# q and k transposed before the launch, first heads' operands written in place, half of the probabilities' low parts queued behind the next row maximum

## The chip, the cores and the metric

The kernel runs on one core of a Trainium2 chip. The metric is the device time of one execution in microseconds (us), taken as the median of several runs. Five engines are named by the profile: PE (matmul; PEld is its weight load), DVE (vector), ACT (scalar), POOL (GpSimd) and SP, which only issues DMAs here. Each engine works through its own instructions in order and waits for others on semaphores.

## The reference, cut to what matters

The program computes an attention in which a query sees only the keys of its own hash bucket, then a mixture of experts with the best expert alone, then a dense layer with ELU. Only the attention is touched by the change. There are 2 batches of 8 heads, 768 positions and 64 dimensions per head; `proj` is 64 by 6.

```
q_bits = (einsum('bhsd,dk->bhsk', q, proj) > 0)       # 6 bits
k_bits = (einsum('bhsd,dk->bhsk', k, proj) > 0)
q_bucket, k_bucket = sum(bits * 2 ** arange(6))
mask = q_bucket[:, :, :, None] == k_bucket[:, :, None, :]
scores = where(mask, q @ k.T / 8, -1e9)
attn = softmax(scores);  attn_out = attn @ v
x = moe(attn_out as [1536, 512]);  out = elu(x @ w_in) @ w_out
```

All values are 32-bit floats. PE multiplies them in a shorter form, so the kernel splits each operand into a high part (the value rounded to that form) and a low part (the value less its high part) and multiplies the parts.

## The kernel before

**Tiles.** The 16 heads are worked as 8 pairs. A head has 6 query tiles of 128 rows, so there are 96 tiles (NQ) and 12 per pair (s = 0 to 11). One trip of the loop over n (lines 951 to 1007) issues, for different tiles, one step of each stage. The order in which the code issues is the order in which each engine works; nothing is rescheduled. A trip issues:

- stage_M(n-1), lines 360 to 370: DVE takes the row maximum `nm` of the scores of tile n-1 out of PSUM, POOL makes a scale `sc` and a bias `bi` of it.
- what was put in the list `early` by the trip before.
- stage_T(n-3), lines 384 to 401: PE turns the probabilities in two halves of 3 blocks (tile `t`, from a PSUM pool of 3 buffers, tag "t"); ACT writes the high part `pthi` and DVE the low part `ptlo` of each half.
- `late[0]`, the first half of a preparation step (below).
- stage_S(n), lines 342 to 353: PE makes the scores `s` by 4 matmuls of 384 columns.
- stage_R, lines 472 to 517, in two trips of twelve: PE brings finished head outputs back into token order by 6 matmuls, DVE scales them.
- stage_V, lines 405 to 415: PE multiplies `pthi` and `ptlo` with v by 4 matmuls (tile `o`).
- stage_E(n-1), lines 372 to 380: ACT takes the exponential of the scores with bias and scale, into `p`.
- stage_O once in three trips: ACT copies `o` out.
- `late[1]`, the second half of a preparation step.
- what the table `todo` has for this trip.

**Mask.** The bucket test is part of the score matmul. The operands are stacked: `qa` holds high and low part of q, `ka` the high part of k twice; `qb` and `kb` hold q's high and k's low part in rows 0 to 63 and, from row 64 on, rows built from the hash bits, so that equal buckets add the large constant UNIT (line 20) and others less. MROWS (line 22) is the number of those rows.

**Preparation of a pair.** While pair pr is worked, the next pair is prepared in 6 steps (lines 994 to 997: at s = 1, 2, 4, 5, 7, 8). Steps 0 to 3 are prep_T (lines 204 to 227), one for each half of 384 positions of q and of k: PE turns three 128x128 blocks of the raw rows (`prep`, PSUM, tag "t"), ACT writes the high part (`qhi`, `khi`), DVE the low part (`qlo`, `klo`). Steps 4 and 5 are prep_Z (lines 273 to 292): 4 matmuls with the projection (`zps`, tag "t"), ACT copies half of the result (`zb`), DVE compares (`z`). restack (lines 294 to 318) then copies the parts to the stacked operands by DMAs on SP's queue. PE, which issues in order, works a step's transposes between stage_V and the next stage_T.

**Start.** Lines 621 to 668 prepare the first pair before the first tile: `load_pair` brings q and k with 64 values in a row of a head, PE turns them, and the first head's operands are copied into their places by ACT, POOL and DMAs. keep_warm issues matmuls without a use.

## Time and profile before

| what | value |
| --- | --- |
| time, median of 3 runs | 712.68 us (712.56 to 712.94) |
| the profiled execution's own time | 713.77 us |
| its span, first to last instruction | 712.0 us |
| first row maximum, that of tile 0 | starts at 10.35 us |
| last row maximum, that of tile 95 | starts at 244.72 us |
| granted TensorE clock, mean | 0.997 |

The 96 tiles thus take a third of the span; what follows (experts, dense layer) is the other two thirds. The rows of the trace that the prediction uses are shown further down. A PE row's duration is longer than the time until the next matmul may start, since matmuls overlap; so on PE the distance from start to start is what counts.

### The profile page before, as it was taken

How to read it: one execution, taken by the hardware profiler on the slowest of the kernel's cores; microseconds unless marked ns; L12 is line 12 of the kernel's file. 1: busy time of each engine (PE TensorE's matmuls, PEld its weight loads, DVE VectorE, ACT ScalarE, POOL GpSimd, SP SyncE). 2: the span in 40 equal slices, each digit the busy share in tenths (PEclk: the TensorE clock that was granted, in tenths of full speed). 3: DMA queues.
4: the chain of work that ended last, by engine and by line, in shares of the span. 5: the costliest groups of instructions: out<-in, count | busy, mean ns of one | idle time of the engine just before them, and what ended most of it. 6: DMA issues, size and time to landing. Idle time of an engine off the chain costs nothing.

```text
span 712.0 us, 12226 instructions
## 1 busy us (share of the span) xinstructions
PE 698.5 (98%) x4211; PEld 626.8 (88%) x4212; DVE 553.7 (78%) x1046; ACT 428.4 (60%) x855; POOL 211.1 (30%) x508
## 2 busy tenths in 40 slices
PE   8999999999999999999999999999999999999996
PEld 6899999999998988999999998788888888888884
DVE  6989898899998997788888887877788547934433
ACT  6988888888888865666666665445443224422221
POOL 7665445455456661221065311000000000002012
PEclk9999999999999999999999999999999999999998
DMA  8857758686691239788878986322222000001011
GB/s 188 198 136 178 186 129 210 163 189 164 144 233 57 84 116 299 239 261 242 261 209 247 256 217 144 104 88 75 89 87 92 2 0 1 0 1 60 0 60 62
DMA packets 108596, 97.39 MB, mean 137 GB/s; under 512 B 33480, under 2 KB 94728, under 8 KB 108528
## 3 DMA queue, kind: packets, MB, share of 16 engines
q1 hardware_dynamic: 106064, 90.15, 47.3%
q0 software_dynamic: 2304, 6.40, 2.4%
q8 instruction: 35, 0.57, 0.3%
q14 instruction: 33, 0.27, 0.1%
q10 hardware_dynamic: 160, 0.00, 0.0%
HBM read 64.15 MB, written 10.72 MB: 105 GB/s over the span
## 4 chain that ended last, share of the span: by engine, by line
issue 32%; PE 23%; DMA 6%; POOL 1%; ACT 0%; SPq 0%; POOLq 0%; ACTq 0%
PE hps L1135 11%; PE yps L1148 7%; DMA out_dram<-part,tidt 5%; PE yps L1150 3%; DMA xs<-xs_d 1%; PE xTp L1117 1%; DMA tidt<-tid_d 1%; PE yps L1147 0%; POOL xs L857 0%; POOL out_dram L1293 0%; ACT sum L1153 0%; POOL spacer L612 0%; SPq L743 0%; POOLq L1293 0%; ACTq L1153 0%
## 5 line engine op out<-in xcount | busy, mean ns | idle before, releaser
L399 DVE TENSOR_TENSOR ptlo<-t,pthi 128x384 fp32r<-128x384 f32 x192 | 99.9, 548 | 14.7 <-ACT pthi L398 13.1
L376 ACT ACTIVATE p<-s,bi,sc 128x768 f32<-128x768 f32 x96 | 95.9, 999 | 17.5 <-POOL bi L369 15.7
L832 DVE TENSOR_TENSOR wl<-wraw,wh 128x1024 fp32r<-128x1024 f32 (+1 forms) x65 | 77.4, 1194 | 23.7 <-ACT wh L828 21.4
L367 DVE TENSOR_REDUCE nm<-s 128x1 f32<-128x768 f32 x96 | 90.9, 947 | 0.3 <-PE s L349 0.3
L398 ACT ACTIVATE pthi<-t 128x384 fp32r<-128x384 f32 x192 | 84.8, 497 | 10.2 <-PE t L396 8.9
L1293 POOL DMA_INDIRECT out_dram<-part,tidt x12 | 11.5, 960 | 263.5 <-DVE part L1290 262.2
L1255 ACT ACTIVATE ee<-gps 128x512 f32<-128x512 f32 x48 | 28.7, 597 | 98.0 <-PE gps L1245 98.0
L1148 PE MATMUL yps<-h,wh 128*128 128x448 f32 x256 | 84.4, 380 | 0.0
L396 PE MATMUL t<-ident,p 128*128 128x128 f32 x576 | 79.5, 273 | 0.0
L1245 PE MATMUL gps<-x2h,vl 128*128 128x512 f32 x192 | 75.9, 395 | 0.0
L1275 PE MATMUL a<-vh,gh 128*128 128x512 f32 x192 | 75.6, 394 | 0.0
L1275 PE MATMUL a<-vh,gl 128*128 128x512 f32 x192 | 75.4, 393 | 0.0
L1245 PE MATMUL gps<-x2h,vh 128*128 128x512 f32 x192 | 75.3, 392 | 0.0
L1245 PE MATMUL gps<-x2l,vh 128*128 128x512 f32 x192 | 75.2, 392 | 0.0
L1275 PE MATMUL a<-vl,gh 128*128 128x512 f32 x192 | 74.9, 390 | 0.0
L349 PE MATMUL s<-ka,qa 128*128 128x384 f32 x192 | 73.4, 383 | 1.2 <-DMA qa<-qlo 0.4
L1258 ACT ACTIVATE gh<-ee 128x512 fp32r<-128x512 f32 x48 | 30.4, 633 | 69.2 <-DVE ee L1257 69.2
L1256 DVE TENSOR_SCALAR ee<-ee 128x512 f32<-128x512 f32 x48 | 20.4, 426 | 66.3 <-ACT ee L1255 66.2
L396 PEld LDWEIGHTS t<-ident,p 128*128 128x128 f32 x576 | 67.4, 140 | 3.9 <-DVE ptlo L399 0.5
L828 ACT ACTIVATE wh<-wraw 128x1024 fp32r<-128x1024 f32 x63 | 66.2, 1052 | 2.7 <-DMA wraw<-in_moe_w_dram 2.7
L413 PE MATMUL o<-pthi,vst 128*128 128x384 f32 x192 | 66.9, 349 | 0.3
L349 PE MATMUL s<-kb,qb 102*128 102x384 f32 x192 | 65.3, 341 | 0.4 <-DMA kb<-z 0.4
(224 smaller groups left out, 1768.8 us busy)
## 6 DMA issues: line engine op xcount, KB each, us to landing
wraw<-in_moe_w_dram SPq DMA_DIRECT2D x64, 512.0 KB
w<-in_moe_w_in_dram SPq DMA_DIRECT2D x16, 512.0 KB
w<-in_moe_w_out_dram SPq DMA_DIRECT2D x16, 512.0 KB
ka<-khi SPq DMA_DIRECT2D x30, 192.0 KB
xs_d<-zt SPq DMA_DIRECT2D x8, 528.0 KB
xs<-xs_d SPq DMA_DIRECT2D x8, 528.0 KB
...
```

Source lines behind the costliest of these rows:

```text
L349: nc.tensor.matmul(ps[:, j, 0:HC], opnd[st, "q" + x][0:n1, cb], opnd[st, "k" + x][0:n1, j * HC:(j + 1) * HC], start=(x == "a"), stop=(x == ...
L367: nc.vector.tensor_reduce(nm, sps[n][:, :, 0:HC], AX.XY, ALU.max, negate=True)
L376: nc.scalar.activation(p.rearrange("p (a b) -> p a b", a=2), sps.pop(n)[:, :, 0:HC], AF.Exp, bias=bi, scale=sc, accum_out=sums[hd][:, c:c ...
L396: nc.tensor.transpose(ps[:, a, :], p[:, kt * 128:(kt + 1) * 128], ident)
L398: nc.scalar.activation(ho, ps, AF.Copy)
L399: nc.vector.tensor_tensor(lo[:, HALF * g:HALF * (g + 1), i * 128:(i + 1) * 128], ps, ho, ALU.subtract)
L413: nc.tensor.matmul(ops[m], vst[hd][:, kt, :], t[:, kt, :], start=(kt == 0 and x == 0), stop=(kt == NC - 1 and x == 1))
L832: fs = [lambda c=slice(j, j + h): eng.tensor_tensor(lo[:, c], r[:, c], hi[:, c], ALU.subtract) for j in range(0, PW, h)]
L1135: nc.tensor.matmul(ps, w[:, dc, fs], x[:, dc], start=(i == 0), stop=(i == len(terms) - 1))
L1148: nc.tensor.matmul(ps, wh[:, f], h[:, :, f], start=(f == 0), stop=last)
L1245: nc.tensor.matmul(ps, w[:, dc], x[:, dc, th * TC:(th + 1) * TC], start=(dc == 0 and i == 0), stop=(dc == KD - 1 and i == 2),)
L1275: nc.tensor.matmul(ps, x[:, cs], w, start=(fb in first_fb and i == 0), stop=(fb in last_fb and i == 2))
```

## The change

1. **Layout from the host.** `kernel()` hands q and k over as [batch, head, 64, 768], with positions in the order in which the tiles use them, and `proj` twice over. prep_T has no transposes: its source is the raw SBUF tile, and ACT and DVE read that in place of PSUM. A pair's q or k is one DMA of 128 rows of 3 KB, in place of two with pieces of 256 bytes.
2. **Start.** The first two heads (0 and 1) get loads of their own (`load_one`). Their high and low parts are written straight into the stacked operands, head by head, by ACT, DVE and POOL; no restack DMA is needed for them. Their hash is taken from the stacked operands with 2 matmuls per operand and stretch in place of 3. Head 1 is done in trips 1 to 4 through `todo`.
3. **Mask rows.** MROWS goes from 38 to 18; restack of the bits takes 2 DMAs per head in place of 3.
4. **Preparation steps.** They are spread by a table to at most one per trip: from the second prepared pair on, the four high parts come at s = 0, 1, 4 and 6, the low parts two trips after the call, ahead of stage_T's, and prep_Z at s = 3 and 7. stage_R comes one trip later (s = 8 and 11).
5. **Low parts.** Of the two `ptlo` of a tile, the second is put in `lows_t` and issued in the next trip, behind stage_M.

```
@@ load_pair @@
-                t = ap2.tile([128, NC, 2 * D], F32, tag="raw_" + nm, name="raw_" + nm, bufs=2 if nm == "q" else 1)
-                step = HALF if pr == 0 else NC
-                for c0 in range(0, NC, step):
-                    for hh in range(2):
-                        nc.sync.dma_start(
-                            t[:, c0:c0 + step, hh * D:(hh + 1) * D],
-                            src[b, h0 + hh].rearrange("(p c) d -> p c d", c=NC)[:, c0:c0 + step],
-                        )
+                t = ap2.tile([128, S], F32, tag="raw_" + nm, name="raw_" + nm, bufs=2 if nm == "q" else 1)
+                nc.sync.dma_start(t, src[b, h0:h0 + 2].rearrange("h d s -> (h d) s"))
@@ prep_T @@
-        r = raw[pr, nm]
-        ps = prep_psum("prep")
-        for c in range(HALF):
-            cc = HALF * j + c
-            nc.tensor.transpose(ps[:, c * 128:(c + 1) * 128], r[:, cc, :], ident)
         sl = slice(j * HC, (j + 1) * HC)
-        sc = 1.0 / float(D) ** 0.5 / UNIT
+        ps = raw[pr, nm][:, sl]
+        sc = SCALE
...
@@ the first two heads @@
+    def key_low(hd, j):
+        o, h = (opnd[hd, t][0:64, half(j)] for t in ("kb", "ka"))
+        nc.vector.tensor_tensor(o, one[hd, "k"][:, half(j)], h, ALU.subtract)
+    def query_low(hd, c0, c1):
+        cs = slice(c0, c1)
+        t = opnd[hd, "qa"]
+        nc.vector.scalar_tensor_tensor(t[64:128, cs], one[hd, "q"][:, cs], SCALE, t[0:64, cs], ALU.mult, ALU.subtract)
+    def hash_of(ps, hd, nm, cs, start=True, stop=True):
+        a = opnd[hd, nm + "a"]
+        w, t = (1, a) if nm == "q" else (2 + hd, opnd[hd, "kb"])
+        m = ps.shape[0]
+        nc.tensor.matmul(ps, bdr[:, w - 1 if nm == "q" else w, 0:m], a[:, cs], start=start, stop=False)
+        nc.tensor.matmul(ps, bdr[0:64, w, 0:m], t[0:64, cs], start=False, stop=stop)
...
@@ stage_T @@
-            nc.vector.tensor_tensor(lo[:, HALF * g:HALF * (g + 1), i * 128:(i + 1) * 128], ps, ho, ALU.subtract)
+            po = lo[:, HALF * g:HALF * (g + 1), i * 128:(i + 1) * 128]
+            if g and later:
+                lows_t.append(lambda: nc.vector.tensor_tensor(po, ps, ho, ALU.subtract))
+            else:
+                nc.vector.tensor_tensor(po, ps, ho, ALU.subtract)
@@ prep, and the table of steps @@
+    def prep(pr, nm, j):
+        high, low = prep_T(pr, nm, j)
+        highs.append(high)
+        early.append(lambda: early.append(low))
...
+            else ((-1, "q", 0), (0, "k", 0), (3, "q", 1), (5, "k", 1))
...
+        for j, n in enumerate((6, 8) if p == 1 else (3, 7)):
+            at(n0 + n, prep_Z, p, j)
@@ the loop @@
         if 1 <= n < NQ + 1:
             stage_M(n - 1)
+        both(lows_t)
+        lows_t.clear()
         stage_A(n)
-        both(early)
-        early = []
+        now, early[:] = early[:], []
+        both(now)
         if 3 <= n < NQ + 3:
             m, part = divmod(n - 5, HALF)
-            stage_T(n - 3, (lambda: stage_G2(m)) if m >= 0 and part == 0 else None)
+            stage_T(n - 3, n < NQ, (lambda: stage_G2(m)) if m >= 0 and part == 0 else None)
...
-        m, part = divmod(n - 13, HALF)
+        m, part = divmod(n - (14 if n < NQ - 12 else 13), HALF)
@@ kernel() @@
+        if name in ("q", "k"):
+            b, h, t, d = a.shape
+            a = a.reshape(b, h, 128, t // 128, d).transpose(0, 1, 4, 3, 2).reshape(b, h, d, t)
```

What moves on the engines is seen in their instruction orders. On PE, in a trip of the loop with a preparation step, before the change (`prep` is the preparation's PSUM tile, `t` the turned probabilities, `s` the scores, `o` the product with v):

```order
L212 MATMUL prep<-ident,raw_k 128x128 x3
L396 MATMUL t<-ident,p 128x128 x6
L349 MATMUL s<-ka_142,qa_140 128x384
L349 MATMUL s<-kb_143,qb_141 128x384
L349 MATMUL s<-ka_142,qa_140 128x384
L349 MATMUL s<-kb_143,qb_141 128x384
L413 MATMUL o<-pthi,vst 128x384
L413 MATMUL o<-ptlo,vst 128x384
L413 MATMUL o<-pthi,vst 128x384
L413 MATMUL o<-ptlo,vst 128x384
```

And PE in such a trip now:

```order
L433 MATMUL t<-ident,p 128x128 x6
L384 MATMUL s<-ka_128,qa_126 128x384
L384 MATMUL s<-kb_129,qb_127 128x384
L384 MATMUL s<-ka_128,qa_126 128x384
L384 MATMUL s<-kb_129,qb_127 128x384
L454 MATMUL o<-pthi,vst 128x384
L454 MATMUL o<-ptlo,vst 128x384
L454 MATMUL o<-pthi,vst 128x384
L454 MATMUL o<-ptlo,vst 128x384
```

The three transposes of the preparation are gone, and nothing stands in their place.

On DVE, two trips of the loop before (`nm` is the maximum, `ptlo` the low part of the turned probabilities, `ri` a reciprocal, `qlo` a low part of the next pair):

```order
L367 TENSOR_REDUCE nm<-s 128x1
L399 TENSOR_TENSOR ptlo<-t,pthi 128x3x128
L460 RECIPROCAL ri<-sm 128x3
L399 TENSOR_TENSOR ptlo<-t,pthi 128x3x128
L221 SCALAR_TENSOR_TENSOR qlo<-prep,qhi 128x384
L367 TENSOR_REDUCE nm<-s 128x1
L399 TENSOR_TENSOR ptlo<-t,pthi 128x3x128 x2
L221 SCALAR_TENSOR_TENSOR qlo<-prep,qhi 128x384
```

And DVE now, two trips (line 438 is the second `ptlo`, put off from the trip before, line 440 the first of its own trip):

```order
L402 TENSOR_REDUCE nm<-s 128x1
L438 TENSOR_TENSOR ptlo<-t,pthi 128x3x128
L223 SCALAR_TENSOR_TENSOR qlo<-raw_q,qhi 128x384
L440 TENSOR_TENSOR ptlo<-t,pthi 128x3x128
L402 TENSOR_REDUCE nm<-s 128x1
L438 TENSOR_TENSOR ptlo<-t,pthi 128x3x128
L225 TENSOR_TENSOR klo<-raw_k,khi 128x384
L440 TENSOR_TENSOR ptlo<-t,pthi 128x3x128
```

One `ptlo` of a tile has moved from ahead of the next maximum to behind it, and the preparation's low part reads SBUF (`raw_q`) where it read PSUM (`prep`).

On DVE at the start, from the first maximum on, before:

```order
L367 TENSOR_REDUCE nm<-s 128x1
L221 SCALAR_TENSOR_TENSOR qlo<-prep,qhi 128x384
L367 TENSOR_REDUCE nm<-s 128x1
L251 TENSOR_SCALAR qb_129<-zps,thr,amp 38x384
L258 TENSOR_SCALAR z<-zps 128x384
L367 TENSOR_REDUCE nm<-s 128x1
L399 TENSOR_TENSOR ptlo<-t,pthi 128x3x128 x2
L258 TENSOR_SCALAR z<-zps 128x384
L367 TENSOR_REDUCE nm<-s 128x1
```

And now (`kb_129` and `qa_126` are operands of head 1, `qb_123` of head 0):

```order
L402 TENSOR_REDUCE nm<-s 128x1 x2
L282 TENSOR_SCALAR qb_123<-zps,thr,amp 18x384
L246 TENSOR_TENSOR kb_129<-kr,ka_128 64x384
L402 TENSOR_REDUCE nm<-s 128x1
L440 TENSOR_TENSOR ptlo<-t,pthi 128x3x128
L261 SCALAR_TENSOR_TENSOR qa_126<-qr,qa_126 64x384
L246 TENSOR_TENSOR kb_129<-kr,ka_128 64x384
L402 TENSOR_REDUCE nm<-s 128x1
L438 TENSOR_TENSOR ptlo<-t,pthi 128x3x128
L293 TENSOR_SCALAR z<-zps 50x384
L440 TENSOR_TENSOR ptlo<-t,pthi 128x3x128
L261 SCALAR_TENSOR_TENSOR qa_126<-qr,qa_126 64x384
```

Head 1's low parts, four instructions of 64x384, now stand between the first maxima, where before one low part of 128x384 stood there for both heads.

## Rows read from the trace of the kernel before

**Rows 1.** The page: busy time, share, instructions; granted clock in 40 slices.
```profile
PE 698.5 (98%) x4211; PEld 626.8 (88%) x4212; DVE 553.7 (78%) x1046; ACT 428.4 (60%) x855; POOL 211.1 (30%) x508
...
PEclk9999999999999999999999999999999999999998
```

**Rows 2.** Windows of pairs 3 and 7: length, then busy PE, PEld, DVE, ACT, POOL.
```profile
67.68:97.46 29.78, 29.78 (x201) 28.84 (x201) 26.84 (x51) 26.13 (x58) 14.77 (x47) 1.00 0.74 186
...
187.38:217.97 30.59, 30.47 (x216) 29.06 (x215) 28.07 (x66) 26.61 (x60) 15.43 (x50) 1.00 0.69 178
```

**Rows 3.** Timeline, PE alone, tiles 24 to 28: start, duration, engine, line.
```profile
66.72 0.42 PE L349 MATMUL s<-ka,qa 128*128 128x384 f32 x1
...
68.81 0.45 PE L349 MATMUL s<-ka,qa 128*128 128x384 f32 x1
...
70.33 0.49 PE L212 MATMUL prep<-ident,raw_q 128*128 128x128 f32 x3
...
70.66 0.82 PE L396 MATMUL t<-ident,p 128*128 128x128 f32 x6
...
71.23 0.42 PE L349 MATMUL s<-ka,qa 128*128 128x384 f32 x1
...
73.64 0.42 PE L349 MATMUL s<-ka,qa 128*128 128x384 f32 x1
...
75.95 0.44 PE L349 MATMUL s<-ka,qa 128*128 128x384 f32 x1
```

**Rows 4.** Groups by line, PE: count, busy us, mean ns.
```profile
L212 PE MATMUL prep<-ident,raw_k 128*128 128x128 f32 x48 | 8.2, 282 | 0.1
L212 PE MATMUL prep<-ident,raw_q 128*128 128x128 f32 x48 | 7.9, 273 | 0.7 <-DMA raw_q<-in_q_dram 0.5
```

**Rows 5.** Timeline, DVE and ACT, tiles 24 to 26.
```profile
67.25 1.02 DVE L399 TENSOR_TENSOR ptlo<-t,pthi 128x384 fp32r<-128x384 f32 x2 [0.18 <-ACT pthi L398]
...
67.68 0.99 ACT L376 ACTIVATE p<-s,bi,sc 128x768 f32<-128x768 f32 x1
...
68.19 0.95 DVE L367 TENSOR_REDUCE nm<-s 128x1 f32<-128x768 f32 x1
...
68.74 0.87 ACT L398 ACTIVATE pthi<-t 128x384 fp32r<-128x384 f32 x2
...
72.71 0.55 DVE L221 SCALAR_TENSOR_TENSOR qlo<-prep,qhi 128x384 fp32r<-128x384 f32 x1
...
73.18 0.95 DVE L367 TENSOR_REDUCE nm<-s 128x1 f32<-128x768 f32 x1
```

**Rows 6.** Timeline, PE and DVE, tiles 31 and 32, which hold stage_R and prep_Z.
```profile
83.10 0.45 PE L349 MATMUL s<-ka,qa 128*128 128x384 f32 x1
...
83.74 0.34 PE L349 MATMUL s<-kb,qb 102*128 102x384 f32 x1
...
84.54 0.95 DVE L367 TENSOR_REDUCE nm<-s 128x1 f32<-128x768 f32 x1
...
86.70 0.42 PE L349 MATMUL s<-ka,qa 128*128 128x384 f32 x1
...
88.36 0.95 DVE L367 TENSOR_REDUCE nm<-s 128x1 f32<-128x768 f32 x1
```

**Rows 7.** Timeline, the start: first transposes, maxima of tiles 0 and 12.
```profile
4.34 0.85 PE L212 MATMUL prep<-ident,raw_k 128*128 128x128 f32 x3
...
10.35 0.96 DVE L367 TENSOR_REDUCE nm<-s 128x1 f32<-128x768 f32 x1 [0.31 <-PE s L349]
...
37.76 0.95 DVE L367 TENSOR_REDUCE nm<-s 128x1 f32<-128x768 f32 x1
```

**Rows 8.** Timeline, DVE instructions with two SBUF inputs, and POOL beside them.
```profile
258.23 0.92 POOL L873 TENSOR_SCALAR sel<-ranks,row 128x224 fp32r<-128x224 bf16 x1 [1.12 <-DVE row L863]
258.35 0.94 DVE L883 SCALAR_TENSOR_TENSOR xlo<-xw,xhi 128x512 fp32r<-128x512 f32 x1
...
259.46 0.74 DVE L883 SCALAR_TENSOR_TENSOR xlo<-xw,xhi 128x512 fp32r<-128x512 f32 x1
```

271 lines of the change are left out of this document (146 added, 125 removed).

## The prediction

> **What bounds the kernel now.** I read the page first, then one window per pair of heads, then the timeline of a few trips of the loop. The page gives the granted clock at nine tenths or more in all forty slices and PE busy for 98% of the span, DVE 78%, ACT 60% [rows 1]. So PE is the engine to doubt first, but its busy time overstates it, because matmul rows overlap. The windows show what the attention looks like by itself: in pair 3 PE is busy for the whole 29.78 us, DVE for 26.84, ACT for 26.13; in pair 7 DVE has risen to 28.07 of 30.59 [rows 2]. Three engines are near full, so taking work from one can hand the bound to the next.
>
> The timeline settles which it is. From the first score matmul of one tile to that of the next takes 68.81 − 66.72 = 2.09 us in a plain trip and 71.23 − 68.81 = 2.42, then 73.64 − 71.23 = 2.41, in trips that hold a preparation step [rows 3]. The three transposes of that step start at 70.33 and the next work starts at 70.66: 0.33 us, exactly the difference [rows 3]. A trip with stage_R and one prep_Z takes 86.70 − 83.10 = 3.60 [rows 6], 1.51 over a plain one. A whole pair is 12 × 2.09 + 4 × 0.33 + 2 × 1.51 = 29.42, against 29.78 in its window [rows 2]: PE's own work explains all but 0.36 us. Part of that rest is seen: the trip from 73.64 to 75.95 has no extra work on PE and yet takes 2.31 [rows 3]. It is the trip that has a high part on ACT and a low part on DVE to catch up with.
>
> **Term 1, the transposes.** They go without a substitute on PE. There are 48 for k and 48 for q in the run [rows 4], 12 per pair. The first pair's 12 belong to the start; the other seven pairs have 28 steps of 0.33 us: 9.2 us. Since the trips with a step are longer by just this, I count it in full, and put what comes late next into term 2. The other bound is zero, if ACT or DVE hold the pace (first rival).
>
> The high and low parts remain, in the same number, now from SBUF. The nearest rows: a low part of 384 columns from PSUM took 0.55 us [rows 5], one of 512 columns from SBUF 0.74 when POOL left it alone [rows 8], which is 0.55 for 384. I take no difference. The bounds are 0.1 either way for 28 of each, on engines which have 2 to 3 us to spare in a pair.
>
> **Term 2, what PE waits for afterwards.** Without transposes a pair is 28.10 us of PE work.
> - ACT: an exponential starts at 67.68, the next instruction at 68.74, and that one takes 0.87 for both halves [rows 5]: about 1.93 a tile. With one further copy of some 0.4 it is above 2.09 for a trip, but the change puts at most one in a trip and gives them the four long trips to recover. On average it fits.
> - DVE: the two low parts take 68.19 − 67.25 = 0.94, the maximum 0.95 [rows 5], together 1.89. Its busy time of 26.84 fits in 28.10, but the 28.07 of pair 7, where gate work is added, does not fit with any slack [rows 2].
> - The put-off low part. It brings the maximum, the bias and the exponential forward by about 0.47 us, so some of the 0.36 us of idle time in a pair should go: half of 7 × 0.36, minus 1.3 us.
> - The same move holds a PSUM buffer longer. The pool of turned probabilities has three. After a trip with stage_R or prep_Z, which takes the third, the second half of the next stage_T needs the buffer that the put-off low part still reads. A trip with one of these is 2.09 + 0.75 = 2.84 long, and that half starts about 0.33 before its end, 2.51 after the scores' start. The maximum can start when the last score matmul ends, 84.08 − 83.10 = 0.98 after it [rows 6]; with 0.95 and 0.5 for maximum and low part the buffer is free at 2.43. It just fits. Today these maxima start 1.44 and 1.66 after the scores' start, behind both low parts [rows 6]; less one low part, that is 0.97 and 1.19. The second leaves PE waiting for 0.13. With 4 such trips a pair and 7 pairs, 28 × 0.07 = plus 2.0 us.
> - DVE's full load in the two pairs with gate work: plus 0.5 us.
>
> Term 2 is −1.3 + 2.0 + 0.5 = plus 1.2 us. Its bounds are −2.5 (all idle time goes) and +6.7 (the first rival).
>
> **Term 3, the start.** The first maximum starts at 10.35 us, 6 us behind the first transposes at 4.34 [rows 7]. Now the parts are made straight from what the DMA brought. In front of the first maximum DVE has two low parts of k (0.94 at the step of two `ptlo`), three pieces of q's (768 columns together, 1.0), three small ones for the hash weights (estimated at 0.7), and three comparisons over 1152 columns (1.5 at the maximum's 0.95 for 768), which wait for PE for about 0.5. Begun where the transposes begin now, 4.34, that ends at 9.0, so 1.3 us early. But the DVE orders show what follows: head 1's parts are made apart from head 0's, three more low parts between the first maxima, of 384 columns each, which I price at the step of a `ptlo`. 3 × 0.47 = 1.4 takes the lead back before tile 12, whose maximum now starts at 37.76 [rows 7]. I take zero, with bounds of −2 (DVE idles there anyway) and +1.5 (the lead isn't there and the three come on top).
>
> Fewer and larger DMAs for q and k, and two in place of three for each head's bits, take time from SP's queue and the DMA engines only; nothing in the windows of the pairs waits for them, so they count zero. So do the fewer mask rows: a score matmul has as many columns as before. In the last pair nothing is prepared, and moving one low part is worth −0.7 to +0.7; I take zero. Experts and dense layer are the same instructions and move as a block.
>
> **Sum.** −9.2 + 1.2 + 0 = −8.0 us. The profiled execution took 713.77 us, which would become 705.8. The runs' median, 712.68, stands 1.1 below that execution, so I forecast 704.7 us. Its own range is 700 to 708.
>
> **Rivals.**
> 1. PE was only just the bound, and DVE and ACT take over. For it speaks the 2.31 us trip without work on PE, and DVE's 28.07. Against it: trips with a step last longer by exactly their transposes. At 2.31 for the six trips with a step of vector or scalar work, 2.09 for two, 2.84 for four, a pair is 29.4: 0.36 less than now, 7 × 0.36 = 2.5 us, so 710.2 us. Chance 0.15.
> 2. Slower: the put-off low part blocks the PSUM pool. Place: the second half of stage_T behind stage_R or prep_Z. If the maxima there start no earlier than now (1.44 and 1.66, mean 1.55), the buffer comes at 1.55 + 0.95 + 0.5 = 3.0 and PE waits 0.5 in 28 trips, 14 us against the 9.2 saved: 717.5 us. It decides once the wait passes 9.2 / 28 = 0.33 us, that is from maxima at 1.4 us behind the scores' start. Against it: DVE has one low part less in front. Chance 0.09.
> 3. DVE and POOL block each other. A low part on DVE with both inputs in SBUF took 0.94 us beside a POOL instruction and 0.74 without one [rows 8]. The 28 low parts of q and k now become such instructions, and they stand close behind a maximum, just when POOL makes the bias that the exponential waits for. If POOL then waits for a low part of 0.55 in half the cases, 28 × 0.27 = 7.7 us are lost again: 712.4 us. The Trainium skill, "SBUF — State Buffer", section "Who interferes with whom", says that a vector instruction with two SBUF inputs contends with a GpSimd instruction that reads SBUF, and that the one which came first holds the port to its end. By that rule POOL could stand for a whole low part each time; the trace agrees in kind with its 0.2 us. Against it: the exponential has some slack now that the maximum is earlier. Chance 0.06.
> 4. More than forecast: the idle time goes altogether and the start keeps its lead, 9.2 + 2.5 + 2 = 13.7, so 699.0. Chance 0.04.
>
> The forecast has the rest, 0.66. The range for 8 in 10 runs from 698.5 to 710.5: the likeliest case, the fourth and most of the first. A measurement of this kernel tells about 0.2%, 1.4 us, from no change. Faster by more than that: the forecast, the fourth and most of the first rival, 0.83. Within it: the third and the rest of the first, 0.08. Slower: the second, 0.09.
>
> **What the profile of the changed kernel would show.** Term 1 is right if scores follow scores at 2.1 us in the trips at s = 1, 2, 4 and 5, and if a pair's window is near 28.5 us; 29.3 or more means the first rival. In a pair's window, DVE's and ACT's busy time should stay as now. The buffer's wait shows as idle time of PE's weight load in front of line 433, released by DVE's line 438, right behind trips 3, 7, 8 and 11: 0.1 us each is term 2, over 0.33 the second rival. The third shows in bias instructions of POOL that start late behind a maximum, and in low parts of q and k over 0.6 us. For the start, the first maximum should stand near 9 us and that of tile 12 between 35.5 and 37.8, the transposes of the second pair being gone there as well. The forecast is wrong if a pair doesn't get shorter by over 0.8 us, or if the stretch behind the last maximum changes its length by over a microsecond.

## The result and the profile after

The changed kernel takes 718.75 us (median of 5 runs, 717.99 to 721.42), the kernel before 712.68 beside it (712.56 to 713.18). The ratio is 1.009, with a 95% interval of 1.0071 to 1.011: 6.1 us slower, where 8 us faster was forecast, and above the range. The profiled execution took 718.75 us, its span is 716.8; the span before was 712.0. (The profiled execution of the kernel before was 1.1 us above its median, so the spans differ by 4.8 us and the medians by 6.1.)

First the page after [rows 1]: busy time by engine, and the granted clock in 40 slices.

```profile
PE 696.7 (97%) x4116; PEld 618.8 (86%) x4117; DVE 560.2 (78%) x1052; ACT 427.3 (60%) x853; POOL 217.3 (30%) x508
...
PEclk7999999999999999999999999999999999999999
```

PE's busy time fell by 1.8 us only, and the clock's first slice is at 7. Then the two windows of [rows 2], pairs 3 and 7, with the same columns.

```profile
75.18:104.23 29.05, 29.00 (x190) 27.41 (x189) 27.02 (x51) 25.93 (x60) 16.02 (x46) 1.00 0.68 182
191.80:224.22 32.42, 29.57 (x201) 27.30 (x200) 28.66 (x66) 26.45 (x61) 16.51 (x48) 1.00 0.67 171
```

Pair 3 gained 0.73 us, against 1.3 forecast; pair 7 lost 1.83. Last the start [rows 7]: the maxima of tiles 0 and 12 on DVE.

```profile
11.31 0.96 DVE L402 TENSOR_REDUCE nm<-s 128x1 f32<-128x768 f32 x1 [0.57 <-PE s L384]
...
45.46 0.96 DVE L402 TENSOR_REDUCE nm<-s 128x1 f32<-128x768 f32 x1 [1.07 <-PE s L384]
```

Tile 0 is 0.96 us late, tile 12 7.70. From tile to tile the account closes: up to tile 12's exponential +8.75 us (39.53 to 48.28), pairs 2 to 6 −4.32, pair 7 +1.98, the last pair −0.98, behind its last exponential −0.63: +4.80, the difference of the spans. (From here on a pair is measured from the exponential of its first tile to that of the next pair's, so pair 7 goes from 30.43 to 32.41.) So there are three questions: what the start lost, what pair 7 lost, and why the plain pairs, 2 to 6, gained 0.86 us each where the forecast comes to 1.14 (8.0 over the seven pairs that hold preparation steps).

Windows of 5 us show the start: length, then busy time of PE, PEld, DVE, ACT, POOL, then the granted clock.

```profile
5.00:10.00 5.00, 2.70 (x9) 1.16 (x10) 4.07 (x10) 1.76 (x4) 1.78 (x3) 0.73 0.92 295
10.00:15.00 5.00, 4.46 (x13) 2.98 (x13) 3.02 (x5) 1.49 (x3) 0.68 (x4) 0.50 0.15 55
15.00:20.00 5.00, 4.67 (x20) 3.42 (x18) 4.69 (x8) 3.35 (x7) 3.62 (x13) 0.75 0.00 0
20.00:25.00 5.00, 4.49 (x27) 3.24 (x26) 4.95 (x11) 3.67 (x9) 4.36 (x13) 1.00 0.00 0
25.00:30.00 5.00, 3.16 (x13) 2.69 (x12) 3.21 (x6) 3.10 (x7) 2.86 (x7) 0.78 0.47 136
```

PE is busy for 2.70 us from 5 to 10 us and for 3.16 from 25 to 30, and in the clock's records the lower level (1.2 GHz) stands from 7.31 to 17.55 us and from 27.79 to 31.2. The kernel before had the full clock from its first record at 5.06 us on, with PE busy for 4.45 and 5.00 us in the same two windows. Two of PE's waits in the start:

```profile
27.67 0.55 PE L384 MATMUL s<-kb,qb 82*128 82x384 f32 x1 [1.22 <-DMA kb<-z]
...
44.65 0.42 PE L384 MATMUL s<-kb,qb 82*128 82x384 f32 x1 [0.94 <-POOL vst L363]
```

Both are the first scores of a new head or pair (tiles 6 and 12), with their `ka` matmul done. The second names POOL, but the bits in the `kb` rows of that tile come from a DMA that SP issued at 41.89 us, 2.8 us before, as those of tile 6 were issued 2.5 before; that this was the wait is read from that distance.

In pair 7, around tile 75, PE and DVE:

```profile
199.83 0.18 DVE L599 TENSOR_TENSOR g_rk<-sp,ohs 128x24 f32<-128x24 f32 x1 [0.96 <-PE sp L598]
...
200.07 0.55 PE L433 MATMUL t<-ident,p 128*128 128x128 f32 x3 [0.28 <-DVE g_rk L599]
...
201.40 0.55 PE L433 MATMUL t<-ident,p 128*128 128x128 f32 x3 [0.78 <-DVE ptlo L438]
```

The gate's ranking (`sp`, from the pool of the turned probabilities), prep_Z and the turned probabilities with a put-off low part ask for three buffers in one trip; DVE and PE wait for each other by turns. From tile 74's exponential to tile 75's it takes 4.22 us, and 4.51 around tile 83, where it is stage_R in place of prep_Z.

In the plain pairs DVE and POOL stand beside each other like this, after the change:

```profile
114.97 0.55 DVE L223 SCALAR_TENSOR_TENSOR qlo<-raw_q,qhi 128x384 fp32r<-128x384 f32 x1
...
115.00 0.57 POOL L404 TENSOR_TENSOR bi<-sc,nm 128x1 f32<-128x1 f32 x1
```

The bias took 0.57 us beside a low part that now reads SBUF; 0.19 is its usual time. This is so beside each of the 28 low parts of q and k (28 of 96 biases, 0.39 to 0.57 us); the low parts themselves all took 0.54 or 0.55.

What PE waits for in a plain pair is seen on its weight load (PEld), here in pair 4 at s = 0, 3 and 6, with ACT ahead of the last:

```profile
105.37 0.19 PEld L384 LDWEIGHTS s<-ka,qa 128*128 128x128 f32 x1 [0.24 <-ACT p L411]
...
112.29 0.31 PEld L433 LDWEIGHTS t<-ident,p 128*128 128x128 f32 x3 [0.23 <-issue]
...
117.70 0.54 ACT L219 ACTIVATE khi<-raw_k 128x384 fp32r<-128x384 f32 x1
...
118.11 1.01 ACT L411 ACTIVATE p<-s,bi,sc 128x768 f32<-128x768 f32 x1
...
119.26 0.19 PEld L384 LDWEIGHTS s<-ka,qa 128*128 128x128 f32 x1 [0.27 <-ACT p L411]
```

The scores wait for the exponential that frees their PSUM, 0.24, 0.16 and 0.27 us at s = 0, 4 and 6, and in each of these trips a high part of 0.53 to 0.54 us stands directly in front of that exponential on ACT. The 0.23 us at line 433 end 0.12 us after a put-off low part that ran from 111.62 to 112.17, in the trip of the first prep_Z (s = 3).

### The profile page after: what moved, and what is told of

It reads as the page before. It is cut to its first block, busy times and chain, and to the rows that moved or that the text cites. A ratio compares the mean times of both kernels' runs of the same rounds, so it can differ in the third digit from the quotient of the medians.

```text
span 716.8 us, 12080 instructions
## 1 busy us (share of the span) xinstructions
PE 696.7 (97%) x4116; PEld 618.8 (86%) x4117; DVE 560.2 (78%) x1052; ACT 427.3 (60%) x853; POOL 217.3 (30%) x508
## 4 chain that ended last, share of the span: by engine, by line
PE 49%; issue 33%; DMA 7%; DVE 5%; ACT 2%; POOL 2%; SPq 0%; DVEq 0%; POOLq 0%; ACTq 0%
PE hps L1180 11%; PE s L384 9%; PE o L454 8%; PE yps L1193 7%; PE t L433 7%; DMA out_dram<-part,tidt 5%; PE yps L1195 3%; PE sp L530 2%; DVE nm L402 1%; PE zps L315 1%; ACT p L411 1%; PE xTp L1162 1%; DMA xs<-xs_d 1%; DVE ptlo L438 1%; DMA xs_d<-xlast,g_idx 1%
## 5 line engine op out<-in xcount | busy, mean ns | idle before, releaser
L433 PE MATMUL t<-ident,p 128*128 128x128 f32 x576 | 82.1, 275 | 2.9 <-DVE ptlo L438 2.3
L384 PE MATMUL s<-ka,qa 128*128 128x384 f32 x192 | 75.3, 393 | 2.3 <-ACT p L411 1.9
L384 PE MATMUL s<-kb,qb 82*128 82x384 f32 x192 | 66.7, 348 | 2.2 <-DMA kb<-z 1.2
L454 PE MATMUL o<-ptlo,vst 128*128 128x384 f32 x192 | 65.4, 341 | 0.0
```

The costliest lines, as they stand in the source:

```text
L384: nc.tensor.matmul(ps[:, j, 0:HC], opnd[st, "q" + x][0:n1, cb], opnd[st, "k" + x][0:n1, j * HC:(j + 1) * HC], start=(x == "a"), stop=(x == ...
L433: nc.tensor.transpose(ps[:, a, :], p[:, kt * 128:(kt + 1) * 128], ident)
L454: nc.tensor.matmul(ops[m], vst[hd][:, kt, :], t[:, kt, :], start=(kt == 0 and x == 0), stop=(kt == NC - 1 and x == 1))
```

## The experiments

All ratios are against the kernel before on the same chip, with 95% intervals. "Plain pair" is pair 4 (tiles 36 to 47).

| run | tile 12's maximum | plain pair | pair 7 | run, us | ratio |
|---|---|---|---|---|---|
| before | 37.76 | 29.78 | 30.43 | 712.68 | |
| after | 45.46 | 29.07 | 32.41 | 718.75 | 1.009 (1.0071–1.011) |
| a_fill | 43.61 | 29.07 | 32.66 | 718.2 | 1.007 (1.0057–1.0084) |
| a_fillwide | 45.10 | 29.05 | 32.66 | 718.89 | 1.0083 (1.0069–1.0096) |
| a_early | 39.87 | 29.08 | 32.39 | 714.42 | 1.0017 (1.0008–1.0026) |
| a_pair7 | 40.32 | 29.07 | 30.11 | 712.04 | 0.9985 (0.9974–0.9996) |
| a_rank | 45.94 | 29.07 | 31.87 | 720.74 | 1.01 (1.0084–1.0116) |
| a_nodefer | 46.31 | 29.53 | 31.45 | 721.93 | 1.0122 (1.0104–1.014) |
| b_layout | 40.30 | 29.54 | 30.26 | 712.58 | 0.9988 (0.9979–0.9998) |
| b_lf | 38.92 | 29.55 | 30.26 | 712.08 | 0.9984 (0.9975–0.9993) |
| b_ldf | 38.45 | 29.93 | 31.14 | 714.8 | 1.0021 (1.0012–1.003) |
| b_pe | 38.68 | 31.01 | 31.37 | 721.02 | 1.0115 (1.01–1.013) |
| b_pe2 | 38.81 | 29.98 | 30.53 | 714.58 | 1.0019 (1.001–1.0028) |
| a_pe2 | 42.11 | 30.02 | 30.27 | 716.17 | 1.0046 (1.0032–1.006) |
| a_lowlate | 40.92 | 30.51 | 30.64 | 720.57 | 1.0106 (1.0091–1.0121) |
| c_best | 38.23 | 29.45 | 30.10 | 713.67 | 1.001 (0.9998–1.0023) |
| c_pe | 39.36 | 33.15 | 31.04 | 729.48 | 1.0227 (1.0213–1.024) |
| c_two | 38.51 | 29.07 | 30.12 | 710.6 | 0.9959 (0.9946–0.9973) |

### The start

**a_fill.** More matmuls that only fill PE's idle time at the start.

```diff
-    keep_warm(12)
+    keep_warm(19)
...
     first_Zq(0, 0, 128)
+    keep_warm(6)
...
+    for i in range(5):
+        at(1 + i, keep_warm, 6 if i == 4 else 3)
```

> The changed kernel with more idle-filling matmuls at the start: 19 in place of 12 ahead of the first hash, 2 behind the second half's key hash, 6 behind the first query hash, 3 in each of the trips 1 to 4 and 6 in trip 5. Nothing else differs. Theory (the granted clock is a large part of the 7.7 us lost before tile 12's maximum): the clock stays at 1.0 or falls for under 4 us in the first 35 us, where the changed kernel had 0.5 for 10.2 and 3.4 us; score matmuls of tiles 0 to 2 step at 0.175 us in place of 0.32; the maximum of tile 6 starts at 25.5 to 27 in place of 28.90, that of tile 12 at 42 to 43.5 in place of 45.46, the run 715.5 to 717. Rival (the start is set by what DVE, ACT and SP's queue do, PE only waits): the clock is up, and yet tile 12's maximum stands at 45 to 46, because its operands come by DMA at the same time; the run 718 to 719.5.

The clock stayed at full, score matmuls stepped at 0.175 us, and tile 12's maximum came 1.85 us earlier. So the clock is a quarter of the start's loss. That is less than the theory asked: 43.61 at tile 12 and 27.88 at tile 6 lie just outside its ranges, and the run, 718.2, lies in the rival's. The run gained 0.55: 0.9 us was left at the last maximum, since pairs 5 and 7 of that execution were 0.3 longer, and the rest went behind it.

**a_early.** The second head one trip earlier, and the second pair's steps in an order that lets q's pieces go first.

```diff
-        at(3 + i, second_Z, i)
+        at(2 + i, second_Z, i)
...
-            ((3, "q", 0), (4, "k", 0), (5, "q", 1), (6, "k", 1)) if p == 1
+            ((2, "q", 0), (3, "q", 1), (4, "k", 0), (5, "k", 1)) if p == 1
...
-        for j, n in enumerate((6, 8) if p == 1 else (3, 7)):
+        for j, n in enumerate((6, 7) if p == 1 else (3, 7)):
```

> The run a_fill with the second head's preparation one trip earlier throughout, and the second pair's in the order q, q, k, k at trips 2 to 5 and its hash at 6 and 7 (in the changed kernel q, k, q, k at 3 to 6, hash at 6 and 8). Theory (what is left of the start's loss is operands that come late over SP's queue: tile 6's scores wait 1.1 us for the second head's bits, tile 12's 1.1 or more for the second pair's): tile 6's maximum 25.8 to 26.8 in place of 27.88, tile 12's 39.5 to 41.5 in place of 43.61, run 714.5 to 716.5 (a_fill 718.2). Rival (DVE is full in the first six tiles, so moving work forward only moves the wait): tile 3's maximum 0.5 or more later than 18.25, tile 12's 43 to 44, run 717.5 to 719.

As the theory had it: 3.74 us earlier at tile 12, 3.8 us of the run. Of the 3.74, 0.70 stand at tile 0 already (10.55 against 11.25), ahead of the trips that the edit moves, so some 3 us are the edit's; a_pair7, with the same start, has tile 12 at 40.32. SP's queue and PE in this run:

```profile
20.71 0.91 SPq L336 DMA_DIRECT2D qb<-z  x1
21.67 0.77 SPq L336 DMA_DIRECT2D kb<-z  x1
...
24.84 0.42 PE L384 MATMUL s<-ka,qa 128*128 128x384 f32 x1
25.10 0.34 PE L384 MATMUL s<-kb,qb 82*128 82x384 f32 x1
```

and SP's queue after the change:

```profile
24.24 0.91 SPq L336 DMA_DIRECT2D qb<-z  x1
25.20 0.77 SPq L336 DMA_DIRECT2D kb<-z  x1
```

The bits go out 3.5 us earlier, and the `kb` matmul no longer waits. What is left against the kernel before, 2.1 us, arises between tiles 0 and 4 (0.20 late at tile 0, 2.39 at tile 4). There DVE makes the second head's four low parts and two comparisons by themselves, where the kernel before made both heads' in one instruction. That part is read from the timeline and was not tested alone; b_lf, with the old start, stands only 1.16 behind.

**a_fillwide.** a_fill with the hash weights padded from 18 and 50 to 128 columns.

```diff
-    bdr = ap1.tile([128, 4, ZM], F32R, name="bdr")
+    bdr = ap1.tile([128, 4, 128], F32R, name="bdr")
```

> The changed kernel with the idle-filling matmuls of the run a_fill and with the hash weights padded with zero columns to 128, so that the hash matmuls of the first two heads hold 128 weight columns in place of 18 and 50. Theory (a narrow weight load isn't put beside the matmul before it: in a_fill these 16 or so matmuls of 384 columns step at 0.28 to 0.305 us, and their weight loads start with them): with 128 weight columns they step at 0.18, which saves PE 0.45 us in each group of four; tile 0's maximum starts 0.2 to 0.6 earlier than 11.25, tile 12's 0.5 to 1.2 earlier than 43.61; run 717 to 718 (718.2 in a_fill). Rival (the step is set by what the matmul reads or by its position, not by its weights): the steps stay at 0.28 to 0.305 and all times as in a_fill.

Neither: the steps grew, and tile 12's maximum came at 45.10. The hash matmuls' weight loads in a_fill start 0.28 us apart:

```profile
6.95 0.09 PEld L268 LDWEIGHTS zk<-kb,bdr 64*18 64x18 f32 x1 [0.33 <-issue]
7.23 0.09 PEld L267 LDWEIGHTS zk<-ka,bdr 128*18 128x18 f32 x1 [0.19 <-issue]
7.51 0.09 PEld L268 LDWEIGHTS zk<-kb,bdr 64*18 64x18 f32 x1 [0.19 <-issue]
```

and in a_fillwide 0.37:

```profile
7.17 0.18 PEld L269 LDWEIGHTS zk<-kb,bdr 64*128 64x128 f32 x1 [0.24 <-issue]
7.54 0.19 PEld L268 LDWEIGHTS zk<-ka,bdr 128*128 128x128 f32 x1 [0.19 <-POOL ka L243]
7.91 0.18 PEld L269 LDWEIGHTS zk<-kb,bdr 64*128 64x128 f32 x1 [0.18 <-issue]
```

The load is not beside the matmul before it in either kernel, so its width is simply added (0.09 or 0.18 us). These matmuls hold 128 and 64 weight rows by turns; whether that is the cause was not tried.

### Pair 7

**a_rank.** The gate's ranking and what follows it one trip later.

```diff
-                    at(n1 + i, f)
+                    at(n1 + i + (i > 15), f)
```

> The changed kernel with the gate's ranking step and the gate steps behind it one trip later, so that in pair 7 it no longer takes a buffer of the turned probabilities' pool in a trip that also has prep_Z or stage_R. Theory (three buffers asked for in one trip cost pair 7 some 2.4 us): the two waits of PE for the DVE's low part in that pair (0.78 and 1.02 us) go, its window falls from 32.42 to between 29.6 and 30.6, and the run to between 716 and 717.2. Rival (DVE is simply full in pair 7, with gate work on top of its 27 us a pair): the window stays at 31.8 to 32.6, the run at 718.2 to 719.2.

The window fell by 0.54 to 31.87, which is in the rival's range, and not by 2 or more: waits of 0.39 and 0.67 us of PE for DVE's low part stood at two other tiles of the pair. The run is slower than after by 0.1%, inside both intervals; its stretch behind the last maximum was 1.1 us longer.

**a_pair7.** a_early with pair 7 set back: old order of steps, stage_R one trip earlier, no low part put off in its tiles.

```diff
-            stage_T(n - 3, n < NQ, (lambda
+            stage_T(n - 3, n < NQ - 24 or NQ - 12 <= n < NQ, (lambda
...
-        m, part = divmod(n - (14 if n < NQ - 12 else 13), HALF)
+        m, part = divmod(n - (14 if n < NQ - 24 else 13), HALF)
```

> The run a_early with the seventh pair alone set back: its preparation steps in the old order (steps at trips 1, 2, 4, 5 and the hash at 7, 8), stage_R one trip earlier as before, and no low part put off in its twelve tiles. Theory (pair 7 lost 2 us because the gate's ranking, prep_Z or stage_R and a put-off low part ask for the three buffers in the same trip): pair 7's window 30.2 to 30.8 (32.39 in a_early, 30.43 in the kernel before), all other windows as in a_early, run 712 to 713 (a_early 714.4). Rival (the eighth pair's steps made from SBUF beside the gate work fill DVE, whatever the order): window 31.4 to 32.4, run 713.5 to 714.8.

As the theory had it, and below the kernel before's 30.43. The windows of pairs 4 and 7:

```profile
100.83:129.90 29.07, 29.00 (x189) 27.44 (x189) 27.08 (x51) 25.94 (x60) 16.18 (x46) 1.00 0.67 175
186.46:216.57 30.11, 29.23 (x203) 27.51 (x202) 28.15 (x66) 26.30 (x60) 14.54 (x45) 1.00 0.70 180
```

DVE does the same work in pair 7 as before (28.15 us, 28.07 in [rows 2]) and fits: it was not full, it was made to wait. The run sets three things back at once; what the put-off part has of it is seen from the four cells below.

### The plain pairs

**a_nodefer.** The changed kernel with no low part put off.

```diff
-            if g and later:
+            if False:
```

> The changed kernel with both low parts of a tile's turned probabilities in their old place, none put behind the next maximum. Theory (the put-off part gains little in plain pairs and costs in pair 7, where its buffer is held longer): windows of the plain pairs 29.0 to 29.5 (29.05 with it), pair 7 down from 32.42 to 30.5 to 31.5, run 717.5 to 720. Rival A (the put-off part is what gained the plain pairs their 0.7 to 1.0 us): plain pairs 29.5 to 29.8, run 720.5 to 723. Rival B (the put-off part blocks the pool in all pairs): plain pairs 28.3 to 28.7, run 713 to 716.

**b_layout.** The kernel before with the new layout alone.

```diff
-        ps = prep_psum("prep")
-        for c in range(HALF):
-            cc = HALF * j + c
-            nc.tensor.transpose(ps[:, c * 128:(c + 1) * 128], r[:, cc, :], ident)
         sl = slice(j * HC, (j + 1) * HC)
+        ps = raw[pr, nm][:, sl]
```

> The kernel before with only the other layout of q and k: they come from memory already turned, the transposes on PE and their PSUM tiles go, the high and low parts are made from SBUF by the same instructions in the same order. Start, order of steps and masks as before. Theory (the loss sits in the new start and in the gate steps that meet others in pair 7, not in the missing transposes): tile 12's maximum at 36 to 38 (37.76 before), a plain pair 28.7 to 29.3 (29.78 before), the run 705 to 709. Rival (low parts made from SBUF meet POOL there, and DVE and ACT hold the pace): a plain pair 29.4 to 29.8, the run 711 to 713. Third: without the transposes PE is too idle at the start here too, the clock falls to 0.5 and tile 12's maximum comes at 40 or later, run 709 to 713.

**b_lf.** The same with more filler at the start.

```diff
-    keep_warm(10)
+    keep_warm(16)
```

> The run b_layout (kernel before, only the layout of q and k changed, no transposes) with 16 in place of 10 idle-filling matmuls ahead of the first hash. Theory (b_layout's start is 2.5 us behind the kernel before at tile 12 because the granted clock was 0.5 from 8.3 to 15.2 us): clock 1.0 throughout, first maximum 11.0 to 11.6 (12.28), tile 12's 38.8 to 39.6 (40.30), run 711 to 712. Rival (DVE and ACT set the start, the clock only sits in their shade): tile 12's maximum 40 to 40.5, run 712.3 to 713.

**b_ldf.** b_lf with the low part put off behind the next maximum, as in the changed kernel.

```diff
-            nc.vector.tensor_tensor(lo[...], ps, ho, ALU.subtract)
+            if g and later:
+                lows_t.append(lambda: nc.vector.tensor_tensor(po, ps, ho, ALU.subtract))
...
             stage_M(n - 1)
+        both(lows_t)
```

> The run b_lf with the put-off low part: from the kernel before, layout, filled start and the second low part behind the next maximum, but the old order of the preparation's steps and the old start. Theory (the pairs' gain in the changed kernel is mostly the put-off low part, since b_layout gained 0.28 us a plain pair and the changed kernel without it 0.2 to 0.3): plain pairs 28.9 to 29.2 (29.5 in b_layout), pair 7 30.0 to 30.6, run 708 to 709.5. Rival (in the old order of steps the put-off part holds a buffer that prep_Z or stage_R asks for, as in pair 7 of the changed kernel): plain pairs 29.4 or more, run 711 to 713.

Rival A of a_nodefer is right: without the put-off part its plain pair is 29.53. Of b_layout the rival and the third came true. There the transposes' absence brought 0.24 us a plain pair and nothing on the run: the start lost 2.5 (clock 0.5 from 8.3 to 15.2 us; b_lf, at full clock, has 1.4 of it back). The theory of b_ldf fell: the plain pair is in its rival's range (the run, 714.8, is above it), and the put-off part costs 0.38 in the old order. So the four cells are 29.55 with neither (b_lf), 29.93 with the put-off part alone (b_ldf), 29.53 with the new order alone (a_nodefer), 29.07 with both (after). The put-off part gains 0.46 us in the one order and loses 0.38 in the other. But the cells with the new order also have 18 mask rows in place of 38; c_best, below, has both edits with 38 rows, and its plain pairs take 29.45 to 30.56. So the gain stands only where all three meet; 18 rows in the old order were not run.

In pair 7 the same cells are 30.26, 31.14, 31.45 and 32.41: there the put-off part costs 0.9 us in either order, and the new order 1.2 to 1.3 with it or without.

Where the transposes' time went is in b_layout's group of score matmuls on the page: count, busy us, mean ns, idle before, releaser.

```profile
L341 PE MATMUL s<-ka,qa 128*128 128x384 f32 x192 | 74.5, 389 | 5.8 <-ACT p L368 5.2
```

The same group in the kernel before:

```profile
L349 PE MATMUL s<-ka,qa 128*128 128x384 f32 x192 | 73.4, 383 | 1.2 <-DMA qa<-qlo 0.4
```

PE now waits 5.2 us for the exponential that frees the scores' PSUM. From scores to scores in pair 4, the four trips with a step became 0.81 us shorter together (9.65 to 8.84), and the two trips behind them, at s = 3 and 6, 0.57 longer (4.62 to 5.19). In front of the exponential stands the maximum, and in front of that a low part; on ACT itself, at s = 3, a high part of 0.56 us (105.47) stands directly in front of the exponential (105.98). DVE in b_layout:

```profile
103.75 0.75 DVE L213 SCALAR_TENSOR_TENSOR qlo<-raw_q,qhi 128x384 fp32r<-128x384 f32 x1
104.42 0.95 DVE L359 TENSOR_REDUCE nm<-s 128x1 f32<-128x768 f32 x1
```

with POOL's `osb<-o,o` of 1.01 us running from 103.06 to 104.07. The kernel before, in the same place of the next step, DVE and POOL:

```profile
109.63 0.55 DVE L223 TENSOR_TENSOR klo<-prep,khi 128x384 fp32r<-128x384 f32 x1
...
108.78 1.01 POOL L423 TENSOR_TENSOR osb<-o,o 64x384 f32<-64x384 f32 x1
```

From PSUM all 24 low parts of pairs 2 to 7 took 0.55 us, also beside `osb`; from SBUF in b_lf those of trips 2 and 5 took 0.56 to 0.91. Yet this is not the main thing that kept the transposes' time from arriving: in a_nodefer all 28 low parts took 0.54 or 0.55 and all 96 biases 0.19, and its plain pair is 29.53 all the same.

**b_pe and c_pe** put three transposes back into each of the 28 steps of b_lf and c_best (below), into spare columns of the scores' tile.

```diff
+        if pr:
+            spare = sps[max(sps)][:, 0, HC:HC + 128]
+            for c in range(HALF):
+                nc.tensor.transpose(spare, ident, ident)
```

> The run b_lf with three transposes put back into each of the 28 preparation steps of pairs 2 to 8, of a constant matrix into spare columns of the scores' PSUM tile, at the place in PE's order where the removed ones stood, without their PSUM tile and with nothing behind them. Theory (in the old order the exponential, the maximum and the low parts set the pace of these trips, and PE's transposes lay beside them): a plain pair 29.55 to 29.85 (b_lf 29.55, kernel before 29.78), run 712 to 713.5 (b_lf 712.1). Rival (the prediction's first term, PE's own work sets the pace): 0.33 us a step come back, a plain pair 30.7 to 30.9, run 720 to 721.5.

> The run c_best with the same three transposes put back into each of the 28 steps. Theory (with one step a tile and the low part put off, PE is the engine that is never waited past): a plain pair 30.0 to 30.4 against c_best's 29.05, run 5 to 8 us above c_best. Rival (PE has room here too, and DVE with 27 us of work a pair sets the pace): a plain pair below 29.5, run less than 3 us above c_best.

Both landed at or beyond the answer in which PE's work counts in full (31.01 and 33.15 us a plain pair), but another reason is seen on DVE in c_pe:

```profile
101.76 0.96 DVE L363 TENSOR_REDUCE nm<-s 128x1 f32<-128x768 f32 x1 [1.72 <-PE s L207]
```

The maximum waits for the filler, because it lies in the tile that the maximum reads. In b_pe the view names the filler at three maxima only. Neither run can tell PE's share.

**b_pe2 and a_pe2** put them where no other engine waits, into the tile that stage_T's own transposes overwrite next: b_lf and a_pair7 with

```diff
             ps = ps_t.tile([128, HALF, 128], F32, tag="t", name="t")
+            if extra:
+                extra.clear()
+                for a in range(HALF):
+                    nc.tensor.transpose(ps[:, 0, :], ident, ident)
```

> The run b_lf (kernel before, new layout, filled start) with PE's work put back: three transposes of a constant matrix at the head of stage_T in the 28 trips behind a preparation step, where the removed ones stood, into the PSUM tile that the tile's own transposes overwrite next; no other engine waits for them. PE's work is then that of the kernel before, and the one difference left in the pairs is that the high and low parts read SBUF. Theory (PE did set the pace, and the low parts made from SBUF beside GpSimd took back what the transposes gave: 0.91 and 0.85 us in place of 0.55 in b_layout's trips 2 and 5): plain pair 30.5 to 31 (kernel before 29.78, b_lf 29.55), run 719 to 721. Rival (the transposes lay beside DVE's and ACT's work and were free): plain pair 29.5 to 29.9, run 712 to 713.5.

> The run a_pair7 (the changed kernel with filled start, earlier second head and pair 7 set back) with the same three transposes put back into the 28 trips behind a step. Theory (in the new order with the low part put off PE sets the pace and each step's 0.33 us counts): plain pair 30.1 to 30.5 (29.05), run 720 to 722 (712.0). Rival (DVE with 27.0 us of work a pair, or the bias on GpSimd, sets the pace and PE has room): plain pair 29.1 to 29.5, run 712.5 to 715.

PE, b_pe2: the filler and the tile's own transposes, 0.32 apart as the removed ones were [rows 3].

```profile
103.46 0.49 PE L392 MATMUL t<-ident 128*128 128x128 f32 x3
103.78 0.82 PE L395 MATMUL t<-ident,p 128*128 128x128 f32 x6
```

In the old order the rival is nearly right: 9.2 us of PE work put back cost 0.43 a plain pair and 2.5 us of the run (ratio 0.9984 to 1.0019). The plain pair of 29.98 and the run of 714.58 lie just above its ranges, and far below the theory's. In the new order it cost 0.95 a plain pair and some 4 us of the run (0.9985 to 1.0046): nearer to the theory in the plain pair, yet below its 30.1, and far below its 720 for the run. And b_pe2, which has the kernel before's PE work and order with the parts read from SBUF, is 0.20 a plain pair longer than the kernel before, and 0.65 over pairs 2 to 7: that is about what the other source costs with PE's work in place. (Two small things differ besides: the filler takes no PSUM buffer of its own, and q and k come by fewer DMAs.)

**a_lowlate.** a_pair7 with q's and k's low parts one place later on DVE, away from the bias.

```diff
-        early.append(lambda: early.append(low))
+        early.append(lambda: early.append(lambda: highs.append(low)))
```

> The run a_pair7 with the low parts of q and k later on DVE by one low part of the turned probabilities, which reads PSUM, so that GpSimd's bias comes beside that one. Theory (in the changed kernel 23 of 71 bias instructions took 0.50 to 0.58 us in place of 0.19 because a low part with two SBUF inputs was there first, and the exponential waits for them): at most 6 of 71 over 0.3 us, plain pair 28.6 to 28.9 (29.05), run 709.5 to 711. Rival (the exponential has slack there): the bias is at 0.19, but the pair stays at 29.0 to 29.1 and the run at 711.5 to 712.5.

The bias is at 0.19, but for two in the first six tiles, and the run is 8.5 us slower, against both answers: the low parts now meet `osb`. DVE and POOL in this run:

```profile
106.18 1.05 DVE L225 TENSOR_TENSOR klo<-raw_k,khi 128x384 fp32r<-128x384 f32 x1
107.15 0.94 DVE L402 TENSOR_REDUCE nm<-s 128x1 f32<-128x768 f32 x1
...
105.80 1.01 POOL L464 TENSOR_TENSOR osb<-o,o 64x384 f32<-64x384 f32 x1
```

Two low parts a pair are longer by 0.3 to 0.6 us, in front of a maximum. They also stand behind a low part that waits for ACT, and the run does not separate the two. What the slow bias itself costs in the changed kernel stays open.

### The version that the runs point to

**c_best.** b_lf, the low part put off except in pair 7, and the changed kernel's order of steps, stage_R and loads in pairs 2 to 6.

```diff
+    for p in range(2, NPAIR - 1):
+        n0 = 2 * NC * (p - 1)
+        for n, nm, j in ((-1, "q", 0), (0, "k", 0), (3, "q", 1), (5, "k", 1)):
+            at(n0 + n, step, p, nm, j)
+        for j, n in enumerate((3, 7)):
+            at(n0 + n, prep_Z, p, j)
```

> What the runs so far point to: the run b_lf (start of the kernel before, new layout, 16 idle-filling matmuls), with the low part put off everywhere but in pair 7, the changed kernel's order of steps (one a tile, hash away from stage_R) in pairs 2 to 6, the old order in the first pair and in pair 7. Theory (the put-off part gains only in the new order of steps: 29.50 us a plain pair with neither, 29.93 with the put-off part alone, 29.53 with the new order alone, 29.05 with both; the start and pair 7 are better the old way): tile 12's maximum 38.2 to 39, plain pairs 29.0 to 29.1, pair 7 30.2 to 30.6, last pair's 11 tiles 25.4 to 25.7, run 708 to 709.5. Rival (the stretch behind the last maximum or the expert stage gives the gain back): the last maximum is 3 us earlier than in b_lf, but the run stays at 710.5 to 712.

Start, pair 7 and last pair came about as expected, but the plain pairs were uneven (29.45 to 30.56), and the run took 713.67 us, in neither range. POOL and ACT at such a place:

```profile
97.20 1.01 POOL L421 TENSOR_TENSOR osb<-o,o 64x384 f32<-64x384 f32 x1 [3.00 <-DMA o<-o]
...
98.70 0.99 ACT L368 ACTIVATE p<-s,bi,sc 128x768 f32<-128x768 f32 x1 [0.85 <-POOL bi L361]
```

POOL stands before `osb`, whose DMA is queued on SP behind six bit transfers, and the bias stands behind `osb`.

**c_two.** c_best with the changed kernel's 18 mask rows, so four transfers.

```diff
-MROWS = 32 + NBITS
+MROWS = 3 * NBITS
...
-                cp("kb", 64, zt[pr], k0, NBITS)
-                cp("kb", 96, zt[pr], k0, NBITS)
+                cp("kb", 64 + NBITS, zt[pr], k0, 2 * NBITS)
```

> The run c_best with the changed kernel's 18 mask rows, so that a head's bits are two DMAs in place of three. Theory (with the hash steps moved behind, SP's queue holds the o shift back behind the bit restacks: in c_best GpSimd waited 3.0 us for it and the exponential 0.85 us for the bias): plain pairs 29.0 to 29.1, tile 12's maximum 38 to 38.6, last maximum 240 to 241.5, run 709.5 to 711. Rival (the pairs are uneven for another reason, such as the old start's place of the loads): plain pairs 29.4 to 30.5 as in c_best, run 712.5 to 714.

The plain pair, tile 12, the last maximum (240.31) and the run came as expected. It is faster than the kernel before by 0.41% (0.27 to 0.54) and than the changed one by about 1.3%. Pairs 3 and 7:

```profile
69.91:98.94 29.03, 28.95 (x189) 27.41 (x188) 27.02 (x51) 25.94 (x59) 16.20 (x46) 1.00 0.70 187
186.49:216.61 30.12, 29.19 (x201) 27.25 (x200) 27.91 (x65) 26.41 (x61) 15.79 (x49) 1.00 0.68 169
```

## Why the prediction was wrong

**Where it was missed.** Spread over the seven pairs that hold steps, the forecast's −8.0 us is −1.1 up to tile 12, −5.7 in pairs 2 to 6, −1.1 in pair 7 and nothing behind it. Measured were +8.75, −4.32, +1.98 and −1.61. So of the 12.8 us between them, the start, term 3, has 9.9, and pair 7 has 3.1; terms 1 and 2 were 1.4 too good in the plain pairs, and the end was 1.6 better than forecast. The steps that failed are term 3's zero, above all, and term 1's counting in full. That the second rival's 717.5 lies near the measured 718.75 is luck: its 0.5 us of waiting in 28 trips did not come.

**Term 3 (0, bounds −2 to +1.5) failed outright: +7.70 at tile 12.** The first maximum was to come 1.3 us early and came 0.96 late. Three things were left out. PE's own pace: nothing was counted for the matmuls that had no transposes beside them to keep the clock up (1.85, a_fill). The path of the later operands over SP's queue: transfers were counted as zero because "nothing in the windows of the pairs waits for them", but at tiles 6 and 12 the scores do, and the steps ahead of these transfers came later than before (3.74 with a_early, some 3 of it by the edit). And the second head's own parts: three low parts were counted, 1.4, where four low parts and two comparisons stand there; by the timeline they are the most of the remaining 2.1, which no run tested alone.

**Term 1 (−9.2 us) was mis-sized, and the first rival names why.** A trip with a step was longer by its transposes' 0.33 us, and from that the prediction counted all 28. But the trip was only as short as the next engine allowed. Put back where nobody waits, the same PE work is worth 2.5 us in the old order and about 4 in the new one. The first rival's price, 0.36 a pair and 2.5 us of the run, is what b_pe2 against b_lf measured (0.43 and 2.5), and its 2.31 for six trips is 2.34 on average in b_lf (s = 1 to 6). The sign that spoke for it was in [rows 3]: a trip of 2.31 us without extra work on PE. Reading it as a trip that catches up, the prediction gave it 0.15. Such a trip stands twice in a pair, at s = 3 and 6, and PE's weight load waits for the exponential there. In pair 4 these waits are 0.46 us in the kernel before and 1.24 in b_lf, one of 0.26 at s = 4 among them: of the 1.32 us that PE no longer works, it waits 0.78 instead.

**The other source of the parts ("no difference") was wrong too, through the third rival, but it is small.** A low part from SBUF took up to 0.91 (b_lf) and 1.19 us (b_pe) when POOL was there first. In the changed kernel it never did; there POOL's bias took 0.39 to 0.57 when DVE was first (28 of 96). [rows 8] had the effect at 0.2 us. The Trainium skill, "SBUF — State Buffer", section "Who interferes with whom", has it that a vector instruction with two SBUF inputs contends with a GpSimd instruction that reads SBUF, and that the one that issued first keeps the shared port for its whole instruction. Here both orders appear, and the trace agrees in kind in both: `klo` ends 0.42 us behind the `osb` that had started first, and the bias 0.05 behind the `qlo` that had. The price of 7.7 us was not borne out by itself: b_pe2 shows 0.65 for pairs 2 to 7. In a_lowlate, with the low parts beside `osb`, the run lost more than that.

**Term 2.** In the plain pairs the put-off part did more than forecast, 0.46 us a pair (29.53 to 29.07) where 1.3 over seven is 0.19, but only with the new order; the prediction did not see that it costs in the old one. In the last pair, taken at zero, it gained 0.9 (25.41 against a_nodefer's 26.29, from tile 84's exponential to tile 95's). Against that, PE's own work of 28.10 us became 29.07, and the "On average it fits" for ACT is a part of that: three trips a pair are 0.16 to 0.27 us longer by a wait for the exponential, with a high part of 0.54 us, counted at 0.4, in front of it. That is 0.67 us a pair, read from the timeline of pair 4; no run moved the high parts alone. The buffer's wait came in another place than forecast: 0.23 us in the trip of the first prep_Z itself, and in pair 4 no wait of PE behind the long trips names line 438. The second rival, that the put-off part blocks the pool, came true in part in pair 7, where the gate's ranking is a third customer in the same trip. 1.98 us were lost there: 0.9 by the put-off part and 1.2 by the new order with its mask rows, less 0.2 that the layout alone gained (30.43 to 30.26). The prediction's 0.5 was for DVE being full, which a_pair7 shows it isn't.

**The transfers at zero** were wrong in the steady pairs as well: c_best against c_two is over 3 us for two small DMAs a pair, in the order of steps that the change brings. **The tail** held: −0.42 us behind the last maximum.

**The signs that the prediction named** point the same way. Pair 3 got shorter by 0.73, under the 0.8 at which the forecast was to be wrong. Of the scores that the first term asked to be 2.1 apart, those at s = 1, 2 and 5 are (2.14, 2.08 and 2.09 in pair 4) and those at s = 4 are not (2.24); the pair's window is 29.05, between the 28.5 of the forecast and the 29.3 of the first rival. Of the third rival's two signs the late bias came, and the low parts of over 0.6 us did not.
